# Scores and old states of a chunked retention in four 64x64 tiles of TensorE, with y in two banks

## The chip, the cores and the metric

The kernel runs on one core of a Trainium2 chip. The metric is the device time of one execution in microseconds (us); TensorE, VectorE, ScalarE and GpSimd are the core's engines, called PE (and PEld for its weight loads), DVE, ACT and POOL in the profile. All timed runs that are compared here are of the fast state, with a mean granted TensorE clock of 0.990 to 1.0 (below 0.993 only in load_early); one run of the kernel before, of 1494.38 us, was of the slow state and is left out. Two single looks have no state and are marked.

## The reference, cut to what matters

```python
# q, k, v: (4 batches, 8 heads, 768 positions, 64), float32
gamma = 1 - 2.0 ** (-5 - np.arange(H))
for t in range(S):
    state = gamma * state + k[t] (x) v[t]            # 64x64 a head
    y[t]  = 1/sqrt(64) * q[t] @ state
x = y as (3072 tokens, 512)
out = (silu(x @ w_gate) * (x @ w_val)) @ w_out       # d_ff = 1536
```

## The kernel before

The recurrence is cut into chunks of 128 positions. Of each chunk the kernel makes scores (keys x queries, decayed and masked), y as the sum of an attention part inside the chunk and of what the state before the chunk gives, and then the new state. Eight heads are four pairs; a pair's two heads lie in partitions 0-63 and 64-127. The tokens go through the two-layer network in four segments of 768 tokens, each of six chunks. The retention of segments 1 to 3 is done piece by piece between the matrix products of the segment before, in what I call its *down stage* (the second layer; a product there is 12 matmul records of 256 columns, 2.6 us). One such piece, a *step*, is: scores of the next chunk, y of this one, this one's state.

```python
def bank(tag):                       # PSUM has eight banks
    own = {"x": (0, 1), "wz": (2, 3), "s": (4, 5), "st": (6,), "y": (7,)}[tag]
    ...
def scores(c):
    kt, qt = (pairs(t) for t in chunks[c][:2])
    sp = [bank("s") for i in range(2)]
    for n in range(NP):              # 4 pairs
        for i in range(2):           # the pair's heads: 64 rows each
            r = ds(D * i, D)
            nc.tensor.matmul(sp[i][:, ts(n, P)], kt[r, n], qt[r, n], start=True, stop=True, ...)
    ...                              # VectorE: times the mask, into a[0], a[1]
def mix(c):
    ...
    if ci:                           # old states' part of y
        for n in range(NP):
            for i in range(2):
                r = ds(D * i, D)
                nc.tensor.matmul(y[r, ts(n, P)], prev[r, n], qd[r, n], start=(n == 0), ...)
    for n in range(NP):              # attention part
        for i in range(2):
            nc.tensor.matmul(y[ds(D * i, D), ts(n, P)], vn[:, ts(2 * n + i, D)], a[i][:, n], ...)
    nc.scalar.copy(xT[...], pairs(y))
def retention(s):                    # a step
    ...
        scores(cs[n + 1]); mix(cs[n]); decay(cs[n]); state(cs[n])
    ...
```

A matmul of 64 rows (contraction) and 128 output partitions runs in a 64x128 tile of the array, one of 64 rows and 64 output partitions in a 64x64 tile, one of 128 rows and 64 output partitions in a 128x64 tile.

## Time and profile before

| | before |
|---|---|
| time, median of the first three runs | 723.43 us (723.40 to 723.66) |
| TensorE busy | 707.4 us of a span of 722.3 |
| VectorE, ScalarE, GpSimd busy | 467.1, 239.8, 239.0 us |
| the three down stages with retention in them | 78.22, 74.55, 75.59 us |

The busy shares, the chain and the timeline of one step are in the prediction. Here are the three down stages (I take a stage from its first product's first matmul to the first matmul of the next stage). The view gives for each stretch its length, then busy us and number of instructions for PE, PEld, DVE, ACT and POOL, then the granted clock, the DMA share and GB/s:

```profile
144.20:222.42 78.22, 77.35 (x634) 65.81 (x632) 56.81 (x111) 12.32 (x35) 11.98 (x9) 1.00 0.64 237
320.69:395.24 74.55, 74.55 (x603) 64.20 (x602) 37.80 (x63) 12.80 (x37) 10.19 (x8) 1.00 0.39 131
492.49:568.08 75.59, 75.59 (x603) 64.85 (x602) 37.72 (x63) 12.35 (x35) 11.38 (x9) 1.00 0.38 130
```

By this view, which counts short gaps between pipelined records as busy, TensorE is busy for all of the second and third stretch and for all but 0.9 us of the first, so whatever these stages lose or gain is TensorE's own time.

### The profile page before, as it was taken

To read this page: it belongs to the slowest core of one execution; us is meant where nothing else is said; L and a number is where in the kernel's file an instruction comes from. 1 tells how busy PE (TensorE), PEld (TensorE's weight loads), DVE (VectorE), ACT (ScalarE), POOL (GpSimd) and SP (SyncE) were. 2 spreads that over 40 slices of the span, in tenths; PEclk is the share of its full clock that TensorE was granted. 3 is DMA by queue.
4 is the path that set the end of the run, shared out by engine and by line. 5 is a ranking of instruction groups with operands and counts; after the bars stand their busy time and mean duration, and the time that the engine had idled before them with its cause. 6 is when DMAs were issued, how large, how long until landed. Compare 5 with 4: busy or idle time off the path is not lost.

```text
span 722.3 us, 11724 instructions
## 1 busy us (share of the span) xinstructions
PE 707.4 (98%) x4544; PEld 616.0 (85%) x4544; DVE 467.1 (65%) x836; ACT 239.8 (33%) x484; POOL 239.0 (33%) x147
## 2 busy tenths in 40 slices
PE   7898999999999999999999999999999999999997
PEld 6654555678889999998888999998888999999886
DVE  3888998686858887875355575656652656667420
ACT  2668778411212232421122333331121233243000
POOL 1334444513101727470210445372210072735000
PEclk9999999999999999999999999999999999999999
DMA  9797986805997967742822555550473155530010
GB/s 319 257 375 255 290 289 220 312 15 192 395 347 277 332 206 271 244 164 88 259 92 103 183 202 206 203 177 16 135 260 132 63 196 202 202 132 1 9 51 30
DMA packets 60824, 139.06 MB, mean 193 GB/s; under 512 B 4576, under 2 KB 27616, under 8 KB 60768
## 3 DMA queue, kind: packets, MB, share of 16 engines
q1 hardware_dynamic: 57312, 132.01, 53.1%
q10 hardware_dynamic: 3456, 6.29, 2.3%
q8 instruction: 36, 0.59, 0.3%
q14 instruction: 20, 0.16, 0.1%
HBM read 101.72 MB, written 36.57 MB: 191 GB/s over the span
## 4 chain that ended last, share of the span: by engine, by line
PE 91%; DVE 1%; DMA 1%; ACT 1%; issue 1%; DVEq 0%; ACTq 0%
PE bank L626 40%; PE bank L709 26%; PE bank L515 13%; PE bank L718 4%; PE bank L385 3%; PE bank L446 3%; PE bank L442 2%; PE bank L424 1%; DMA hsp<-in_w_gate_dram 1%; DVE ring L289 0%; DVE iop L591 0%; ACT bank L246 0%; DVE hT L665 0%; ACT loadp L249 0%; DVE ring L261 0%
## 5 line engine op out<-in xcount | busy, mean ns | idle before, releaser
L626 PE MATMUL bank<-loadp,ring 128*128 128x192 f32 x720 | 140.3, 327 | 0.0
L709 PE MATMUL bank<-wot,hsp 128*128 128x256 f32 x576 | 129.8, 382 | 0.0
L709 PEld LDWEIGHTS bank<-wot,hsp 128*128 128x128 f32 x576 | 108.0, 190 | 15.8 <-issue 0.5
L626 PEld LDWEIGHTS bank<-loadp,ring 128*128 128x128 f32 x720 | 120.6, 190 | 1.0 <-ACT midp L591 0.7
L591 DVE TENSOR_TENSOR iop<-bank,iop 128x384 f32<-128x384 f32 x144 | 79.7, 556 | 56.3 <-PE bank L626 52.9
L626 PE MATMUL bank<-xs,ring 128*128 128x192 f32 x432 | 87.9, 326 | 0.0
L661 POOL TENSOR_TENSOR hT<-iop 128x768 f32<-128x768 f32 x36 | 67.0, 1862 | 34.8 <-DVE iop L591 34.8
L591 ACT COPY hsp<-bank 128x384 f32<-128x384 f32 x90 | 42.9, 478 | 100.3 <-PE bank L626 89.6
L626 PEld LDWEIGHTS bank<-xs,ring 128*128 128x128 f32 x432 | 73.2, 190 | 0.0
L591 POOL TENSOR_TENSOR iop<-hsp,midp 128x768 f32<-128x768 f32 x9 | 16.3, 1814 | 165.7 <-ACT hsp L591 137.2
L515 PE MATMUL bank<-xs,ring 128*128 128x384 f32 x192 | 64.7, 488 | 2.6 <-DVE xs L498 1.7
L626 PE MATMUL bank<-xT,ring 128*128 128x192 f32 x324 | 66.2, 327 | 0.7 <-DVE iop L591 0.7
L709 PE MATMUL bank<-wot,hT 128*128 128x256 f32 x288 | 65.5, 381 | 0.0
L515 PEld LDWEIGHTS bank<-xs,ring 128*128 128x128 f32 x192 | 36.1, 190 | 29.4 <-issue 2.3
L709 PEld LDWEIGHTS bank<-wot,hT 128*128 128x128 f32 x288 | 54.3, 190 | 7.6 <-issue 0.2
L626 PE MATMUL bank<-hsp,ring 128*128 128x192 f32 x288 | 56.7, 326 | 0.5 <-ACT hsp L591 0.5
L626 PEld LDWEIGHTS bank<-xT,ring 128*128 128x128 f32 x324 | 54.8, 190 | 2.0 <-DVE iop L591 1.8
L515 PE MATMUL bank<-xT,ring 128*128 128x384 f32 x144 | 49.4, 488 | 1.6 <-DVE hT L552 1.6
L626 PEld LDWEIGHTS bank<-hsp,ring 128*128 128x128 f32 x288 | 48.4, 190 | 0.8 <-ACT hsp L591 0.8
L591 DVE TENSOR_TENSOR midp<-bank,midp 128x384 f32<-128x384 f32 x72 | 39.8, 554 | 13.8 <-PE bank L626 12.4
L768 DVE TENSOR_TENSOR iop<-bank,iop 128x256 f32<-128x256 f32 x12 | 5.1, 424 | 65.1 <-PE bank L709 48.1
L449 ACT COPY xT<-bank 128x512 f32<-128x512 f32 x24 | 14.1, 586 | 97.3 <-PE bank L446 97.3
(146 smaller groups left out, 985.9 us busy)
## 6 DMA issues: line engine op xcount, KB each, us to landing
ring<-unitt SPq DMA_DIRECT2D x50, 896.0 KB, 4.6
unitt<-ring SPq DMA_DIRECT2D x21, 896.0 KB, 6.4
unitb<-ring SPq DMA_DIRECT2D x12, 896.0 KB, 7.2
ring<-unitb SPq DMA_DIRECT2D x21, 512.0 KB, 6.0
out_dram<-iop ACTq DMA_DIRECT2D x24, 256.0 KB, 2.4
loadp<-in_w_val_dram SPq DMA_DIRECT2D x18, 256.0 KB, 3.8
loadp<-in_w_gate_dram SPq DMA_DIRECT2D x9, 512.0 KB, 6.1
midp<-in_w_out_dram SPq DMA_DIRECT2D x12, 256.0 KB, 6.1
```

What stands on the lines that cost most here:

```text
L385: nc.tensor.matmul(sp[i][:, ts(n, P)], kt[r, n], qt[r, n], start=True, stop=True, skip_group_check=True)
L424: nc.tensor.matmul(st[ds(D * i, D), n], kd[:, h], vn[:, h], start=(n == 0), stop=True, skip_group_check=True)
L442: nc.tensor.matmul(y[r, ts(n, P)], prev[r, n], qd[r, n], start=(n == 0), stop=False, skip_group_check=True)
L446: nc.tensor.matmul(y[ds(D * i, D), ts(n, P)], vn[:, ts(2 * n + i, D)], a[i][:, n], start=(ci == 0 and n == 0), stop=True, skip_group_check ...
L449: nc.scalar.copy(xT[:, :, c // NCK % 2, ts(ci % L, P)], pairs(y))
L515: nc.tensor.matmul(o, w[:, slot, k], a[:, k], start=(start and k == 0), stop=(stop and k == KH - 1), skip_group_check=True)
L591: events.append((t, len(events), lambda: fn(*args, **kw)))
L626: nc.tensor.matmul(o[:, h], w[:, h, slot], rhs, start=(start and h == 0), stop=True, skip_group_check=True)
L661: by_block(9.5, 13.5, lambda r: pool(to[:, r], u2[:, r], p5[:, r], op=add))
L709: nc.tensor.matmul(o, a[:, k], wot[k][:, slot], start=(start and k == 0), stop=(k == FH - 1), skip_group_check=True)
L718: nc.tensor.matmul(o, a_dn(0, 0, u)[:, k], wot[k][:, B11], start=(k == 0), stop=(k == FH - 1), skip_group_check=True)
L768: tt(ev[0][:, DH:], wb, u2, op=ALU.add)
```

## The change

The intent: use all four quarters of the array for old states (before, row half 0 went to column half 0 and row half 1 to column half 1), give scores the same tile shape so that the array does not change its mode between the two, and pay for it with a second bank for y and with ScalarE copies that move each head to its place. Comments, blank lines and what the first segment keeps are cut.

```diff
-        own = {"x": (0, 1), "wz": (2, 3), "s": (4, 5), "st": (6,), "y": (7,)}[tag]
+        own = {"s": (4, 5), "y": (6, 7)}[tag]
@@ scores
         for n in range(NP):
-            for i in range(2):
-                r = ds(D * i, D)
-                nc.tensor.matmul(sp[i][:, ts(n, P)], kt[r, n], qt[r, n],
-                                 start=True, stop=True, skip_group_check=True)
+            for m in (slice(None),) if c in first_chunks else (slice(0, D), slice(D, P)):
+                for i in range(2):
+                    r = ds(D * i, D)
+                    nc.tensor.matmul(sp[i][m, ts(n, P)], kt[r, n, m], qt[r, n],
+                                     start=(n == 0), stop=True, skip_group_check=True)
@@ state
-        st = bank("st")[:, : NP * D].rearrange("p (n e) -> p n e", n=NP)
+        st = banks[6 if c in first_chunks[:4] else 3][:, : NP * D]
@@ mix, later segments
+            y = [bank("y")[:, : 2 * P].rearrange("p (b t) -> p b t", b=2) for i in range(2)]
+            own = [(2 * h + b, i, h, y[i][:, b])
+                   for b in range(2) for i in range(2) for h in range(2)]
+        for k, (n, i, h, to) in enumerate(own if ci else []):
+            r = ds(D * i, D)
+            nc.tensor.matmul(to[ds(D * h, D)], prev[r, n], qd[r, n],
+                             start=k < 2 * len(y), stop=False, skip_group_check=True)
...                                      # attention part: same targets
-        nc.scalar.copy(xT[:, :, c // NCK % 2, ts(ci % L, P)], pairs(y))
+            for h in range(2):
+                for i in range(2):
+                    nc.scalar.copy(xT[ds(D * i, D), ds(2 * h, 2), seq, pos],
+                                   y[i][ds(D * h, D)])
@@ down stage, twice
-            z = bank("wz")[:, :DH]
+            z = banks[2][:, :DH]
```

More of the change, by code (lines that the diff above doesn't have):

```diff
@@ L419, in state @@
         new = state_of(c)
-        st = bank("st")[:, : NP * D].rearrange("p (n e) -> p n e", n=NP)
+        st = banks[6 if c in first_chunks[:4] else 3][:, : NP * D]
+        st = st.rearrange("p (n e) -> p n e", n=NP)
         for n in range(NP):
@@ L431, in mix @@
     def mix(c):
-        ci = c % NCK
+        ci, seq, pos = c % NCK, c // NCK % 2, ts(c % L, P)
         qd, vn = pairs(chunks[c][1]), chunks[c][2]
         a = att.pop(c)
-        y = banks[(0, 1, 2, 3, 7, 6)[first_chunks.index(c)]] if c in first_chunks else bank("y")
-        if ci:
-            prev = state_of(c, 1)
-            for n in range(NP):
-                for i in range(2):
-                    r = ds(D * i, D)
-                    nc.tensor.matmul(y[r, ts(n, P)], prev[r, n], qd[r, n],
-                                     start=(n == 0), stop=False, skip_group_check=True)
-        for n in range(NP):
-            for i in range(2):
-                nc.tensor.matmul(y[ds(D * i, D), ts(n, P)], vn[:, ts(2 * n + i, D)],
-                                 a[i][:, n], start=(ci == 0 and n == 0), stop=True,
-                                 skip_group_check=True)
-        nc.scalar.copy(xT[:, :, c // NCK % 2, ts(ci % L, P)], pairs(y))
-        if c in first_chunks:
-            att[c] = pairs(y)
+        prev = state_of(c, 1)
+        if c in first_chunks:
+            y = [pairs(banks[(0, 1, 2, 3, 7, 6)[first_chunks.index(c)]])]
+            own = [(n, i, i, y[0][:, n]) for n in range(NP) for i in range(2)]
+        else:
+            y = [bank("y")[:, : 2 * P].rearrange("p (b t) -> p b t", b=2) for i in range(2)]
[5 more added lines that the diff above has]
+                             start=k < 2 * len(y), stop=False, skip_group_check=True)
+        for k, (n, i, h, to) in enumerate(own):
+            nc.tensor.matmul(to[ds(D * h, D)], vn[:, ts(2 * n + i, D)], a[i][:, n],
+                             start=(ci == 0 and k < 2 * len(y)), stop=True,
+                             skip_group_check=True)
+        if c in first_chunks:
+            att[c] = y[0]
+            nc.scalar.copy(xT[:, :, seq, pos], att[c])
+        else:
+            for h in range(2):
+                for i in range(2):
+                    nc.scalar.copy(xT[ds(D * i, D), ds(2 * h, 2), seq, pos],
+                                   y[i][ds(D * h, D)])
     def retention(s):
@@ L757, in down @@
         cur = dict(hs)
-        wb = bank("wz")[:, :DH]
+        wb = banks[2][:, :DH]
         product(wb, T1, cur[1])
```

## The prediction

> **What bounds the kernel now.** I read the page's busy shares first, then the chain that ended last, then the list of waits, then a timeline of one step of the changed code.
>
> ```profile
> PE 707.4 (98%) x4544; PEld 616.0 (85%) x4544; DVE 467.1 (65%) x836; ACT 239.8 (33%) x484; POOL 239.0 (33%) x147
> PE 91%; DVE 1%; DMA 1%; ACT 1%; issue 1%; DVEq 0%; ACTq 0%
> PE bank L626 40%; PE bank L709 26%; PE bank L515 13%; PE bank L718 4%; PE bank L385 3%; PE bank L446 3%; PE bank L442 2%; PE bank L424 1%; DMA hsp<-in_w_gate_dram 1%; DVE ring L289 0%; DVE iop L591 0%; ACT bank L246 0%; DVE hT L665 0%; ACT loadp L249 0%; DVE ring L261 0%
> ```
>
> TensorE is busy 98% of the span and is 91% of the chain; VectorE and ScalarE have 35% and 67% to spare. Of the lines that the change touches, scores (L385), the attention part of y (L446), the old states' part (L442) and the state update (L424) are together 9% of the chain, some 65 us, and a fair part of it is the first segment, which keeps its instructions. The list of waits has no TensorE entry on these lines that is worth anything over 3.6 us in the whole run. So they cost what their instructions take to stream, plus gaps that are TensorE's own. The gaps show in the timeline of one step (scores of the next chunk, then y of this one, then its state), TensorE matmuls alone; columns are start, length, line, tiles, form, count:
>
> ```profile
> 164.96 0.59 PE L709 MATMUL bank<-wot,hsp 128*128 128x256 f32 x2
> 165.48 1.16 PE L385 MATMUL bank<-loadp 64*128 64x128 f32 x16
> 166.57 1.09 PE L442 MATMUL bank<-loadp,state 64*64 64x128 f32 x16
> 167.59 1.09 PE L446 MATMUL bank<-midp,loadp 128*64 128x128 f32 x16
> 168.52 0.64 PE L424 MATMUL bank<-loadp 128*64 128x64 f32 x16
> 169.08 0.48 PE L709 MATMUL bank<-wot,hT 128*128 128x256 f32 x1
> ```
>
> Each of these calls is two records (16 records for 8 calls), since every f32 product is two matmuls. The view of L442 by duration adds the length of one record, 269 ns as a rule, which is modelled and overlaps the next; so I take starts.
>
> ```profile
> L442 PE MATMUL bank<-loadp,state x160: 269/269/320, 166.6 to 543.8; 64*64 64x128 f32 x160
> L446 PE MATMUL bank<-midp,loadp x192: 272/273/323, 167.6 to 544.8; 128*64 128x128 f32 x192
> ```
>
> From the timeline, L442's last record starts at 166.57+1.09-0.27 = 167.39. The individual records lie in pairs 7 ns apart, one for each head of a pair, and the next pair follows 109 ns later (111 ns in L385). A 256-column product outside takes 216 ns from start to start, 0.84 ns a column, so 128 columns stream in 107-108 ns: two tiles run side by side, and each keeps its own pace. L442's rows 0-63 go to columns 0-63 and rows 64-127 to columns 64-127: half of the array stands idle.
>
> **What the Trainium skill says.** (1) "TensorEngine Tiling (Array Packing)", Key Properties: a change of tiling mode drains TensorE, a change of tile alone doesn't. The trace agrees: L385, L442 and L446 differ in mode, and between the end of one's streaming and the next one's weight load there is 0.09 us each time (L442's last record streams until 167.39+0.11 = 167.50, L446 begins at 167.59), while L446 and L424, of one mode, follow without a gap. After the gap the first weights are not hidden: 0.05 us for 64 columns, 0.11 us for 128 (the first records are 0.05 and 0.10 us longer than the rest). (2) The same page, Restrictions and Gotchas, Gotcha 1: different row tiles may not write one PSUM bank at a time. That is why y now needs two banks; before, the diagonal gave each head its own partitions of one bank. Nothing in this trace tests it. (3) "TensorE: Matmul & The Clock Gate", Part 1: start to start never drops below about 25 ns. Four tiles of 128 columns need 109/4 = 27 ns. The densest stretch of this trace, L424, has 16 records with 58 ns from pair to pair, 29 ns each, so 27 ns is just outside what is shown here. (4) "ScalarE: Activation LUTs", What ACT_TABLE_LOAD costs: an activation with immediates takes 186 ns + 0.833 ns an element; 512 elements give 613, the trace has 586 (below), and 372 for a copy of 256 elements (L722), against 399.
>
> **The change, part by part.** It touches the 18 chunks of segments 1 to 3; the trace has 96 records of L385 in each of these three segments, 64 of L442 in the middle one (its first two chunks have no old state) and 96 in the others.
>
> Scores: 16 records in two 64x128 tiles become 32 in four 64x64 tiles. The streaming per tile is the same, 8 records. Before: gap 0.09, first weights 0.11, 8 x 0.111 = 0.89, sum 1.09 us. After, if four tiles run as freely as two: 0.09 + 0.05 + 8 x 0.109 = 1.02. I choose 115 ns a round of four instead of 109, since 27 ns a record is near the floor: 0.09 + 0.05 + 0.92 = 1.06. Gain 0.03 us each, 18 times: 0.5 us (1.3 at best).
>
> Old states: before 0.09 + 0.05 + 8 x 0.109 = 1.02 us (166.57 less 0.09 to 167.50). After: four tiles, 4 rounds x 0.115 = 0.46, and no gap and no bare weights where scores go before, since both are in 64x64 tiles. Gain 0.56 us. Of the 16 chunks with old states, 13 follow scores; the last of each segment has no scores before it and keeps the gap, gain 0.42. Sum 13 x 0.56 + 3 x 0.42 = 8.5 us.
>
> Attention part of y and states: same number, shape and mode; the state goes to bank 3. Nothing.
>
> ScalarE: one copy of 128x512 becomes four of 64x256, and copies for chunks of the first segment stay.
>
> ```profile
> L449 ACT COPY xT<-bank 128x512 f32<-128x512 f32 x24 | 14.1, 586 | 97.3 <-PE bank L446 97.3
> ```
>
> At 0.37 us each, as a copy of 256 elements takes, four are 1.5 us for 0.59, so up to 0.9 us later for each chunk and at most 16 us more on an engine that is 67% idle. What reads them is the sums of x on VectorE, one 2.6 us product later or more; the decay of the state, behind them on ScalarE, is done at 170.3 in the step above and wanted at 175.5. TensorE's next write into y comes after the state (0.5 us), a product (2.6 us) and the scores (1 us), so 4 us later, and the copies need some 1.5. Beside other work, free.
>
> Banks: the second output half's product and the first's now share bank 2. Between the two there is always a whole product of 2.6 us in bank 0 or 1. VectorE's emptying is late by at most about 1 us where it is busiest:
>
> ```profile
> 217.24 5.34 PE L709 MATMUL bank<-wot,hT 128*128 128x256 f32 x24
> ...
> 220.63 0.42 DVE L729 TENSOR_TENSOR iop<-bank,iop 128x256 f32<-128x256 f32 x1
> ```
>
> The product that L729 empties ends at 219.8, the emptying at 221.05, the next product ends at 222.4. Free, with more than 1 us in hand.
>
> Sum: 0.5 + 8.5 = 9.0 us with my 115 ns, 10.2 us at 109 ns. All of it lies on the chain. 723.4 - 9.0 = 714.4; between the two cases I say 714.
>
> **The rivals.** (a) Four tiles don't run four abreast: issue, or weight loads of tiles with the same rows, hold them to two at a time. Then the 32 records of scores take 16 rounds, 1.75 us for 0.89, 18 x 0.81 = +14.6 us, and only 13 gaps of 0.15 are won: about 736. For it: no stretch of this trace has four tiles. Against it: row tiles (L385) and column tiles (L446) each run side by side here, weights included, and a tile that waits doesn't hold up the other: at 11.36 us the second column tile, which had waited for VectorE, and the first tile's next call start 7 ns apart. With three abreast scores would lose 0.22 us each and old states win 0.44 or 0.29: about 721.
> (b) Another wait takes the place: y's two banks serve one chunk, so four copies must be out before the next y; or one bank for two products. If each of the 16 steps lost 0.5 us, 722. The margins above, 2.5 and 1 us, speak against it.
> (c) The second-level products start earlier than their operands are ready, most of all after the first down stage, where VectorE is busy 57 of 80 us with weight sums and waits up to 3.7 us for their DMA. It would eat at most that stage's third of the gain: 717. Against it: no matmul waits there now, and the sums of the units end some microseconds before they are wanted.
>
> **Range and chances.** The arithmetic allows 10.2 us at most, so 712 is about the floor once run-to-run noise (0.3 us) is added; overheads of issue or (b) or (c) in part give up to 719. Range 711.5 to 719.5. Faster by over 2% would take 14.5 us, more than all that the change can win: 0.02. Slower by over 2% needs all of (a) and something more: 0.03. Within 2%: 0.95.
>
> **What would show it.** In the trace after: L385's 32 records in about 0.9 us and old states' 16 in about 0.45, right behind, with rounds of four starts 109 to 115 ns apart; no 0.09 us gap between them; the gap before the attention part still there; 3.4 us saved in each down stage (2.3 in the middle one); ScalarE up by 10 to 16 us; no wait of TensorE for a copy to xT or for L729. I am wrong if rounds of four take over 150 ns, or if a matmul waits for ScalarE or for bank 2.

## The result, and the profile after

| | before | after |
|---|---|---|
| median, first measurement | 723.54 us (4 runs) | 714.59 us (4 runs, 714.15 to 716.40) |
| ratio of the fast runs | | 0.9873, 95% interval 0.9845 to 0.9901 |
| span of the profiled run | 722.3 us | 712.4 us |
| TensorE busy, records | 707.4 us, 4544 | 698.0 us, 4832 |
| ScalarE busy | 239.8 us | 257.2 us |
| down stages | 78.22, 74.55, 75.59 us | 74.53, 72.03, 71.90 us |
| the rest of the span | 493.92 us | 493.92 us |

Ratios are the mean time of one kernel's fast runs over that of the other's of the same rounds, so not quite the ratio of the medians quoted. The gain is 1.3%: clear of noise, but by the 2% rule of this study the two kernels count as the same. Run times of one kernel vary by more than a microsecond here. Where two traces of one kernel were kept (the changed kernel, causal, copies_x2), the three stages differ by 0.03 to 0.56 us in sum and the rest of the span by 0.1 to 3.8 us. The two traces of the table differ by 9.90 us, and all 9.90 are in the three stages (3.69 + 2.52 + 3.69); that the rest agrees to 0.01 us is a lucky pair (in after_again it is 493.78). The profiled run of before was a slightly long one (724.06 us) and that of after a short one (714.15), hence 8.95 between the medians. For shares of the change I use stage lengths. Those of the second and third stage repeat to 0.01 us; the first varies by half a microsecond, most of it a wait that a second trace, shown below, has.

Page of the changed kernel, busy shares and chain:

```profile
PE 698.0 (98%) x4832; PEld 607.8 (85%) x4832; DVE 467.6 (66%) x836; ACT 257.2 (36%) x538; POOL 239.8 (34%) x147
PE 91%; DVE 1%; DMA 1%; ACT 1%; issue 1%; SPq 0%; DVEq 0%; ACTq 0%
PE bank L640 40%; PE bank L723 27%; PE bank L529 13%; PE bank L732 4%; PE bank L388 3%; PE bank L455 3%; DMA hsp<-in_w_gate_dram 1%; PE bank L428 1%; PE bank L452 1%; DVE ring L290 0%; DVE iop L605 0%; ACT bank L247 0%; DVE hT L679 0%; ACT loadp L250 0%; SPq L221 0%
```

The bound is what it was. Line numbers have moved: scores are L388 now, old states L452 (2% of the chain before, 1% now), attention L455, state L428, the down products L723. The three stages, in the view of the stretches:

```profile
144.19:218.72 74.53, 73.66 (x729) 62.67 (x728) 57.46 (x110) 18.01 (x53) 11.98 (x9) 1.00 0.66 245
317.00:389.03 72.03, 72.03 (x699) 61.90 (x698) 37.15 (x63) 18.67 (x55) 10.25 (x8) 1.00 0.39 136
486.27:558.17 71.90, 71.90 (x698) 61.72 (x697) 37.66 (x63) 18.05 (x53) 11.48 (x9) 1.00 0.38 136
```

TensorE has some 95 records more in each stretch and is done sooner; in this trace no new wait of it appears. ScalarE has 5.7 to 5.9 us more in each. The same step as in the prediction, TensorE's matmuls in the timeline of the changed kernel:

```profile
164.89 0.59 PE L723 MATMUL bank<-wot,hsp 128*128 128x256 f32 x2
165.42 1.10 PE L388 MATMUL bank<-loadp 64*64 64x128 f32 x32
166.34 0.62 PE L452 MATMUL bank<-loadp,state 64*64 64x128 f32 x16
166.89 1.09 PE L455 MATMUL bank<-midp,loadp 128*64 128x128 f32 x16
167.81 0.64 PE L428 MATMUL bank<-loadp 128*64 128x64 f32 x16
168.38 0.48 PE L723 MATMUL bank<-wot,hT 128*128 128x256 f32 x1
```

From the first start of scores to the next product it was 165.48 to 169.08, 3.60 us, and is 165.42 to 168.38, 2.96 us. Thirty-two records of scores take 0.92 us up to old states' first start, and sixteen of old states 0.55 up to the attention part with the gap in it, for 1.02 before. In the single records the four tiles of a round start 7 ns after one another and the next round 109 ns after this one: 27 ns a record, without loss. The waits of TensorE's loads on these lines (columns: us in total, times, longest) hold no ScalarE; the largest are of the kind that the kernel before had, where L385 had 3.6 us and L446 2.9:

```profile
PEld bank L388 <- issue: 4.5, 14, 0.3
PEld bank L455 <- issue: 3.3, 19, 0.2
```

ScalarE's copies in the same step: four in 1.51 us, and the decays behind them.

```profile
167.81 1.51 ACT L464 COPY xT<-bank 64x256 f32<-64x256 f32 x4 [8.33 <-PE bank L455]
169.35 1.06 ACT L414 ACTIVATE state<-state,tab 128x64 f32<-128x64 f32 x4
```

TensorE writes old states into these banks again at 174.68 (the single records), 5.4 us after the last copy has ended.

### The profile page after: what moved, and what is told of

The parts are those of the page before. It is cut to its first block, busy times and chain, and to the rows that moved or that the text cites. A ratio compares the mean times of both kernels' runs of the same rounds, so it can differ in the third digit from the quotient of the medians.

```text
span 712.4 us, 12349 instructions
## 1 busy us (share of the span) xinstructions
PE 698.0 (98%) x4832; PEld 607.8 (85%) x4832; DVE 467.6 (66%) x836; ACT 257.2 (36%) x538; POOL 239.8 (34%) x147
## 4 chain that ended last, share of the span: by engine, by line
PE 91%; DVE 1%; DMA 1%; ACT 1%; issue 1%; SPq 0%; DVEq 0%; ACTq 0%
PE bank L640 40%; PE bank L723 27%; PE bank L529 13%; PE bank L732 4%; PE bank L388 3%; PE bank L455 3%; DMA hsp<-in_w_gate_dram 1%; PE bank L428 1%; PE bank L452 1%; DVE ring L290 0%; DVE iop L605 0%; ACT bank L247 0%; DVE hT L679 0%; ACT loadp L250 0%; SPq L221 0%
## 5 line engine op out<-in xcount | busy, mean ns | idle before, releaser
L723 PE MATMUL bank<-wot,hsp 128*128 128x256 f32 x576 | 129.8, 382 | 0.0
L723 PEld LDWEIGHTS bank<-wot,hsp 128*128 128x128 f32 x576 | 108.0, 190 | 15.9 <-issue 1.0
L529 PE MATMUL bank<-xs,ring 128*128 128x384 f32 x192 | 64.7, 488 | 2.4 <-DVE xs L512 1.7
L723 PE MATMUL bank<-wot,hT 128*128 128x256 f32 x288 | 65.5, 381 | 0.0
L529 PEld LDWEIGHTS bank<-xs,ring 128*128 128x128 f32 x192 | 36.1, 190 | 29.2 <-issue 2.3
L723 PEld LDWEIGHTS bank<-wot,hT 128*128 128x128 f32 x288 | 54.3, 190 | 7.6 <-DVE midp L394 0.2
L640 PEld LDWEIGHTS bank<-xT,ring 128*128 128x128 f32 x324 | 54.8, 190 | 2.0 <-DVE iop L605 1.8
L464 ACT COPY xT<-bank 64x256 f32<-64x256 f32 x72 | 26.4, 366 | 68.3 <-PE bank L455 67.4
L529 PE MATMUL bank<-xT,ring 128*128 128x384 f32 x144 | 49.4, 488 | 1.6 <-DVE hT L566 1.6
L529 PEld LDWEIGHTS bank<-xT,ring 128*128 128x128 f32 x144 | 27.0, 190 | 21.2 <-DVE hT L566 2.2
```

Source lines behind the costliest of these rows:

```text
L464: nc.scalar.copy(xT[ds(D * i, D), ds(2 * h, 2), seq, pos], y[i][ds(D * h, D)])
L529: nc.tensor.matmul(o, w[:, slot, k], a[:, k], start=(start and k == 0), stop=(stop and k == KH - 1), skip_group_check=True)
L640: nc.tensor.matmul(o[:, h], w[:, h, slot], rhs, start=(start and h == 0), stop=True, skip_group_check=True)
L723: nc.tensor.matmul(o, a[:, k], wot[k][:, slot], start=(start and k == 0), stop=(k == FH - 1), skip_group_check=True)
```

## The experiments

All kernels gave correct results. My theory: the 9.9 us are the halved streaming of old states plus TensorE's own gaps and bare weight loads, and the rest of the change is free. The rivals: the gain is mostly in scores; the banks, or the copies, matter; the tiles are only free of one another in a lucky order.

### scores_two: scores back in two tiles

```diff
-            for m in (slice(None),) if c in first_chunks else (slice(0, D), slice(D, P)):
+            for m in (slice(None),):
```

> The changed kernel with scores back in two 64x128 tiles, all else kept. Theory (the gain is streaming of the old states halved, plus TensorE's own gaps): each of 18 scores loses 0.07 us (bare weights of 128 columns again, 111 for 109 ns a round) and the 13 old states that follow scores get back the gap of 0.15 us, so 3.2 us of the 9.9 us between the two traces are lost: about 717.7 us, the three down stages about 1.2, 0.9 and 1.2 us longer than in the changed kernel. Rival (the gain is mostly in scores, or in the banks): nearly all is lost, 723, or nothing, 714.5.

Measured: 717.46 us (6 runs), ratio to before 0.9905 (0.9888 to 0.9922). The stages are 75.68, 72.85 and 73.05 us: 1.15, 0.82 and 1.15 more than in the changed kernel, 3.12 in all, 3.2 expected. A step in its timeline:

```profile
167.43 1.16 PE L388 MATMUL bank<-loadp 64*128 64x128 f32 x16
168.53 0.67 PE L452 MATMUL bank<-loadp,state 64*64 64x128 f32 x16
169.12 1.09 PE L455 MATMUL bank<-midp,loadp 128*64 128x128 f32 x16
```

Scores take 1.10 us up to the next line for 0.92, since the gap is back, and the records of old states take longer again (0.67 for 0.62), for their first weights are bare. So about a third of the gain hangs on scores being in 64x64 tiles, although they stream as long as before. Two things are in that third, and the stages tell them apart: each has six scores, and 5, 3 and 5 of them stand before old states. From 1.15 = 6a + 5b and 0.82 = 6a + 3b, b, the cost of a change of shape before old states, is 0.165 us, 2.1 us in 13 places, and a, scores' own smaller weights and rounds, 0.05 us, 1.0 us in 18 places.

### y_diag: y as before, scores in four tiles

```diff
-            y = [bank("y")[:, : 2 * P].rearrange("p (b t) -> p b t", b=2) for i in range(2)]
-            own = [(2 * h + b, i, h, y[i][:, b]) for b in range(2) for i in range(2) for h in range(2)]
+        y = bank("y")                          # mix() as in the kernel before
+                    nc.tensor.matmul(y[r, ts(n, P)], prev[r, n], qd[r, n], ...)
+        nc.scalar.copy(xT[:, :, c // NCK % 2, ts(ci % L, P)], pairs(y))
```

> The changed kernel with y as before: old states on the diagonal in one bank, one copy of 128x512; scores stay in four tiles. Theory: only the streaming is lost, 16 x 4 rounds x 0.109 = 7.0 us, for diagonal and four tiles are one mode, so no gap comes back: about 721.4 us. The two losses of this run and of scores_two add up to the whole, 10.2 us. Rival (a change of which tiles are used costs as much as a change of mode): another 13 x 0.1 = 1.3 us, 722.7. Rival (the gain is mostly in scores): 715.

Measured: 721.31 us (5 runs), ratio 0.9959 (0.9945 to 0.9974). Stages 77.13, 73.76 and 74.50 us: 2.60, 1.73 and 2.60 more, 6.93 in all, 7.0 expected.

```profile
165.44 1.10 PE L388 MATMUL bank<-loadp 64*64 64x128 f32 x32
166.36 1.05 PE L446 MATMUL bank<-loadp,state 64*64 64x128 f32 x16
167.34 1.09 PE L450 MATMUL bank<-midp,loadp 128*64 128x128 f32 x16
```

Scores and old states follow each other without a gap, so two diagonal tiles and four tiles are one mode; sixteen records in two tiles take 0.98 us up to the attention part for 0.55. The losses of the two runs are 3.12 + 6.93 = 10.05 us, the whole is 9.90: the parts add up, and no part of the gain needs another cause. This run has one copy, the changed kernel four, which is one more sign that the copies are not on the path.

### banks_copies: the old matmuls, the new banks and copies

```diff
# mix() as in y_diag, scores as in scores_two, and
-        nc.scalar.copy(xT[:, :, c // NCK % 2, ts(ci % L, P)], pairs(y))
+            for h in range(2):
+                for i in range(2):
+                    nc.scalar.copy(xT[ds(D * i, D), ds(2 * h, 2), c // NCK % 2, ts(ci % L, P)],
+                                   pairs(y)[ds(D * i, D), ds(2 * h, 2)])
```

> The matmuls of the kernel before, with the banks of the changed one (one bank for two products, the state in bank 3, y in turn in two) and ScalarE's four copies of 64x256. Theory: banks and copies are free, neither cost nor gain: 723.5 us, the down stages as long as before to 0.1 us, ScalarE's busy time up by 14 to 17 us. Rival (the banks of y or of the products were a hidden wait before): down to 720. Rival (the copies cost something): up to 726.

Measured: 724.39 us against 724.30 of before in the same rounds, ratio 1.0005 (0.9992 to 1.0018). The stages are 78.22, 74.54 and 75.59 us, those of before to 0.01. ScalarE is busy 257.6 us, 17.8 more, a little over the range given. Banks and copies in this form neither cost nor bring anything. Here y takes its two banks in turn, one a chunk, while the changed kernel needs both for each chunk, so this run gives the copies more room than they have there; that they are free in the changed kernel too rests on its trace, where no matmul waits for them.

### tile_by_tile: another order of the calls

```diff
-        for n in range(NP):
-            for m in ...:
-                for i in range(2):
+        for m in ...:
+            for i in range(2):
+                for n in range(NP):
+        by_tile = own if c in first_chunks else sorted(own, key=lambda o: (o[1], o[2], o[0]))
+        for k, o in enumerate(by_tile if ci else []):          # old states, tile after tile
```

> The changed kernel with the order of calls changed: scores and old states one tile after another (all calls of a tile in a row) instead of going round the four tiles. Theory A (a tile's queue runs far ahead of the others): nothing changes, 714.5. Theory B (the look-ahead across tiles is short, a few records): tiles run one after the other in whole or in part; with none abreast scores would take 32 x 0.109 = 3.5 us for 0.9 and old states 1.7 for 0.44, 18 x 2.6 + 16 x 1.3 = +68 us, so something between 730 and 782.

Measured: 741.75 us (4 runs), ratio 1.0246 (1.0224 to 1.0268). Stages 83.31, 80.80 and 80.68 us, 8.8 more each. (The first segment's scores are in the new order too; it costs under 1 us there.)

```profile
167.61 2.24 PE L388 MATMUL bank<-loadp 64*64 64x128 f32 x29
169.59 0.35 PE L455 MATMUL bank<-loadp,state 64*64 64x128 f32 x3
169.69 0.27 PE L388 MATMUL bank<-loadp 64*64 64x128 f32 x1
169.75 0.30 PE L455 MATMUL bank<-loadp,state 64*64 64x128 f32 x3
```

Twenty-nine of the 32 records of scores fill the time up to 169.59, and three more come among those of old states, by then on the other three tiles. In the single records, the second tile's first one starts at 168.105, just after the fifth of the first tile (168.099), the third tile's at 168.599, just after the fifth of the second (168.594): a tile's stream is passed only when it has three records left to start. So theory B holds, in the lower part of its range: the look-ahead is real but short. A tile's eight records take 0.87 us and the next tile's start 0.49 us after its own, so that 1.8 tiles run at a time, and in this order the change would have been a loss of 2.5%.

### two_calls: two calls of a tile in a row

```diff
+        runs = ((0,), (1,), (2,), (3,)) if c in first_chunks else ((0, 1), (2, 3))
+        for m, i, ns in [(m, i, ns) for ns in runs for m in ms for i in range(2)]:
+            for n in ns:
+        # old states as in tile_by_tile: each tile has just two calls
```

> The changed kernel with two calls (four records) of a tile in a row before the next tile's turn, in scores and old states of the later segments. In tile_by_tile the second tile began when the first one's fifth record did, so with three of its records waiting. Theory A (each tile may have three or so of its own waiting): four abreast as before, 714.6. Theory B (three or so may wait over all tiles together): the second tile starts at once, the third and fourth 0.2 and 0.3 us later, each section 0.2 to 0.4 us longer, 34 sections: 721 to 728.

Measured: 716.50 us (4 runs), ratio 0.9883 (0.9856 to 0.9909). Stages 75.21, 72.60 and 72.58 us, 0.6 to 0.7 more than in the changed kernel.

```profile
166.07 1.17 PE L390 MATMUL bank<-loadp 64*64 64x128 f32 x32
166.99 0.74 PE L457 MATMUL bank<-loadp,state 64*64 64x128 f32 x16
167.66 1.09 PE L460 MATMUL bank<-midp,loadp 128*64 128x128 f32 x16
```

Scores take 0.92 us up to old states' first start, as in the changed kernel; in the single records the four tiles start 13 ns apart and then keep their 109 ns, with one slip of 0.05 us of three of them at the second turn. So the limit is one of each tile, not of all together, and four records in a row just fit. Theory A holds but for about 0.1 us a step.

### copies_x2, copies_x4 and copies_x2_again: how much room ScalarE has

```diff
-            for h in range(2):
+            for h in list(range(2)) * 2        # and * 4
```

> The changed kernel with each of the four copies of y made twice. Theory (ScalarE has room: in the trace the four take 1.5 us from 167.8 on, and TensorE writes y again at 174.7): no change, 714.6 give or take a run, no wait of TensorE for ScalarE in the down stages. Rival (the copies are near the path): each of 18 steps loses up to 1.5 us, up to 741.

> The changed kernel with each of the four copies of y made four times, 16 copies or 6.1 us a step. Theory: this uses up the room; the copies end at 173.9 in that step, the state's decay behind them at 174.9, its add on VectorE at 175.5, while TensorE wants state and banks at 174.7; products' own copies wait behind them too. One to two us lost in each of about 16 steps: 730 to 747, with TensorE waiting for ScalarE or VectorE. If it is still 714.6, the room is larger than I read it.

Single looks, state unknown. Twice: 715.58 us; the second and third stage are unchanged (72.03 and 71.90), the first is 76.04, 1.51 more. Its timeline near the end of that stage:

```profile
216.87 0.42 DVE L786 TENSOR_TENSOR iop<-bank,iop 128x256 f32<-128x256 f32 x1
...
217.35 1.35 PE L723 MATMUL bank<-wot,hT 128*128 128x256 f32 x5 [0.82 <-DVE iop L786]
```

VectorE's list is long here, and L786, which empties the bank of the next product, stands at the end of it; TensorE waits 0.82 us. A smaller delay of 0.17 us stands 3.7 us earlier, behind L782. In the changed kernel's trace L786 is done at 215.55 and the product that needs the bank starts at 216.1, so 0.6 us are in hand.

Four times: 729.90 us, stages 83.65, 76.60 and 74.07, that is 15.9 more in all. The expectation (1 to 2 us in each of about 16 steps, 730 to 747) is missed by 0.1 us at its low end, and its form is not what happened: three waits make most of it.

```profile
178.72 1.86 PE L723 MATMUL bank<-wot,hsp 128*128 128x256 f32 x6 [2.07 <-DVE iop L743]
```

L743 empties bank 2, the one that two products share now; TensorE stood for 2 us. What follows a little later, in the view of the stretches:

```profile
179.90:182.80 2.90, 2.90 (x8) 2.29 (x7) 1.48 (x3) 2.75 (x9) 0.00 (x0) 0.50 0.95 254
```

The granted clock (the number after the counts) is 0.50 in this stretch, and the single records of products lie 0.43 us apart for 0.22. In the clock records of the trace the half clock lasts from 179.84 to 183.26, 3.4 us, so the wait cost its length and then some 1.7 us more (seven gaps longer by 0.21 and two by less). Two more waits, of 2.61 us (for L786) and 2.21 us (for ScalarE, which empties bank 2 in another product), are followed by 3.4 us of half clock too; the three with what follows are, if each cost 1.7 us more like the first, some 12 of the 15.9 us.

Was it the copies that cost the first stage 1.5 us in copies_x2, or a chance delay? The changed kernel itself, run a second time beside causal_again (below), also had a wait at the same place, 0.46 us beyond the usual distance of two starts, in a first stage of 75.09 us for 74.53, after VectorE had waited for the DMA of weight units:

```profile
210.94 0.69 DVE L171 TENSOR_TENSOR ring<-ring 128x512 f32<-128x512 f32 x1 [3.48 <-DMA ring<-unitb]
...
216.38 0.92 PE L723 MATMUL bank<-wot,hT 128*128 128x256 f32 x3 [0.30 <-DVE iop L786]
```

> The kernel of copies_x2, unaltered. Its first look lost 1.5 us in the first down stage, behind an emptying on VectorE that was late. But after_again, with single copies, has a wait of 0.46 us at the same place, and in both VectorE had waited for the DMA of weight units just before. Theory (the room of ScalarE is enough, the loss was the DMA's): the first stage lies within 74.5 to 75.1 us, as in the changed kernel. Rival (the doubled copies did it): 76.0 again.

Measured: 718.62 us (4 runs), ratio 0.9919 (0.9903 to 0.9936); the first stage is 76.00, with waits of 0.31 and 0.80 us at the same two places. So the rival holds, by two traces against two: the doubled copies did it; how they make VectorE later was not followed further. The rest of this run's extra time lies before the first down stage, where no copy is doubled yet (see the end of the experiments). The copies are free as they are, in two stages even when doubled, but in the first stage there is no room for twice as many.

### load_early: the weight units' loads one ahead

```diff
-            if count[1] < len(to_sum) + 1 and k > 1 and count[1] < 3 + count[2] // 3:
+            if count[1] < len(to_sum) + 1 and k > 1 and count[1] < 4 + count[2] // 3:
```

> The changed kernel with the loads of weight units in the first down stage issued one unit earlier (4 ahead for 3). Theory (VectorE's waits of 1.2 to 3.5 us for these loads make it late for emptying a product's bank, with 0.6 us in hand): the waits shrink, no matmul waits at the end of the stage, 74.5 us for the stage, 714.3 with less scatter. Rival (a load starts when its place in the ring is free, whatever the order): the same waits, the stage 74.5 to 75.1 as before, 714.6.

Measured: 732.38 us (4 runs), ratio 1.0115 (1.0096 to 1.0134); the first stage is 88.99 us, the other two unchanged. Neither expectation is met. VectorE's waits for these loads did not shrink but grew to 22.4 us in all, the longest 7.8 us:

```profile
224.00 0.69 DVE L171 TENSOR_TENSOR ring<-ring 128x512 f32<-128x512 f32 x1 [4.90 <-DMA ring<-unitb]
225.53 0.42 DVE L782 TENSOR_TENSOR iop<-bank,iop 128x256 f32<-128x256 f32 x1
...
226.00 1.22 PE L723 MATMUL bank<-wot,hT 128*128 128x256 f32 x2 [7.90 <-DVE iop L782]
```

The waits of the DMA queue itself between 180 and 228 us show why the loads came later (L161 issues a load, L176 stores a unit that is done); the changed kernel first, then this run:

```profile
SPq L161 <- DMA unitt<-ring: 12.0, 7, 3.6
SPq L161 <- DMA unitt<-ring: 37.0, 6, 7.7
```

A load waits until the unit in its place of the ring is stored. With one load more ahead, the next store stands right behind that waiting load (a load at 205.45, a store at 205.88; 213.19 and 213.65; 219.56 and 220.02), so each load waits for the whole store before it, and the last loads go out 6.4 to 7.7 us apart, for 3.4 to 5.3 in the changed kernel. What the run also shows, much enlarged, is the way from a late load to TensorE: VectorE stands waiting for the load, empties the product's bank late, and TensorE stands still.

### causal, and causal_again beside after_again: a shorter version

Scores of keys 64 to 127 with queries 0 to 63 are multiplied by zeros of the mask. With scores in quarters, these calls can stream half the columns. So that both column halves of the array gain, odd pairs keep their keys with the halves exchanged (a layout of k, v, decays and mask on the host).

```diff
+                    late = c not in first_chunks and (m.start > 0) != (n % 2 > 0)
+                    t = slice(D, P) if late else slice(0, P)
-                    nc.tensor.matmul(sp[i][m, ts(n, P)], kt[r, n, m], qt[r, n],
+                    nc.tensor.matmul(pairs(sp[i])[m, n, t], kt[r, n, m], qt[r, n, t],
```

> The changed kernel, with the scores that the mask zeroes anyway left out: keys 64 to 127 of a chunk need only queries 64 to 127, so half of the 64x64 tiles' calls stream 64 columns for 128. For odd pairs of heads the two halves of the keys change places (rows of k, v, their decays and the mask, laid out so on the host), so that each tile has as many short calls as long ones. Theory (a tile's own stream sets the time, tiles are free of one another): a scores section takes 4 x 0.109 + 4 x 0.058 = 0.67 us for 8 x 0.109 = 0.87, 18 x 0.21 = 3.7 us less than the changed kernel: 710.9, each down stage 1.2 us shorter. Rival (issue is near its limit with four tiles, so shorter streams gain nothing): 714.6, same down stages.

> The kernel of the run causal, unaltered, in the same rounds as the changed kernel: its three down stages were 1.2 us shorter each in the trace, so 3.6 us less than after_again, ratio 0.982 to the kernel before. If it is within 1 us of after_again, the gain of the stages is lost elsewhere.

> The changed kernel itself, unaltered, as the neighbour of causal_again in the same rounds: 714.6 by the first measurement, ratio to the kernel before 0.987.

Measured: causal 712.30 us, ratio to before 0.9840 (0.9820 to 0.9861). In its second time, in the same rounds, 712.68 us and 0.9835 (0.9808 to 0.9862) against after_again's 714.59 us and 0.9854 (0.9832 to 0.9877). Stages of causal: 73.34, 70.81 and 70.68 us, 1.19, 1.22 and 1.22 less than the changed kernel's, as expected (1.2). A step of it:

```profile
165.74 0.90 PE L390 MATMUL bank<-loadp 64*64 64x128 f32 x32
166.46 0.62 PE L454 MATMUL bank<-loadp,state 64*64 64x128 f32 x16
```

Scores take 0.72 us for 0.92. So even rounds of mixed length, 32 records in 0.7 us or 22 ns each, are not held up by issue. In the timed runs the gain over the changed kernel is 1.9 us between the medians, less than the stages' 3.6, and the two intervals overlap; both kernels' runs scatter by 2 to 5 us (causal_again from 710.67 to 715.23). It is the fastest kernel of the study by every median and by the stages, but against the changed kernel the timed difference is not clear of noise. Part of the scatter is the first stage (73.34 and 73.71 us in causal's two traces, 74.53 and 75.09 in the changed kernel's); another part lies before the first down stage, whose first product starts between 143.9 and 147.8 us in the traces of all these kernels. Most of that is there by 36 us: the first product of the network (L515 before, L529 in the changed kernel) starts between 32.3 and 35.3 us, after waits of TensorE in the first segment, a good part of them for loads of q. The latest is copies_x2_again, where one such wait takes 2.86 us, for 1.2 to 1.3 in most of the others, and 3.4 us of half clock follow. Why these loads scatter stays open.

## Why the prediction was right or wrong

The time was right: 714.0 said, 714.59 measured, in the range. Step by step:

- **The bound.** Right. TensorE stayed at 98% and 91% of the chain, and what it saved in the three stages reached the end: the rest of the span is 493.92 us in both traces (to this digit by luck).
- **Scores.** Right in kind, too small. With 115 ns a round I had 0.03 us each; at the measured 109 ns it is 0.07 (1.09 before; 165.325, the end of the last product's streaming, to 166.343 after, 1.02). This is the term that was mis-sized, out of caution about a floor at 25 ns a record that 27 ns did not touch and that causal's 22 ns show to be no floor here. The prediction's own trace spoke against reading that figure across tiles: two tiles' records start 7 ns apart there.
- **Old states.** Right: y_diag gives back 6.93 us, where four rounds of 109 ns saved 16 times are 7.0. The gap between scores and old states went, the one before the attention part stayed (166.80 to 166.89), both as said.
- **The sum.** 9.0 said, 10.2 as the best case; the traces have 9.90, stages 3.69, 2.52 and 3.69 where I said 3.4, 2.3 and 3.4. The same 109 for 115 ns explains it to 0.3 us (208 rounds by 6 ns is 1.2 us). Between the medians it is 8.95, nearer to 9.0 by chance of the runs.
- **Copies.** Free, as said (the changed kernel's trace; banks_copies). ScalarE's extra was 17.4 us, over the 16 of the text. The room was larger than I said: I put one product between a step and the next write into y, there are two, 6.9 us from the first copy's start for 4.
- **Banks.** Free, as said. The narrowest place was not the one that I looked at (bank 2, over 1 us) but the next product's own bank, 0.6 us in hand behind the same list of VectorE, where copies_x2 waits. With four times the copies bank 2 does become a wait, the rival (b) of the prediction. Under (2) the prediction says that nothing in its trace tests the rule on row tiles and banks. The kernel before does in part: in old states rows 0-63 and rows 64-127 write one bank, in different partitions, 7 ns apart, and y_diag does so again with correct results. Four tiles in one bank would also write the same partitions, and no run tries that.
- **The rivals.** (a) fell: four tiles run four abreast. But tile_by_tile shows how near it was: the same calls in another order are rival (a) in part, at 741.75 us where (a) said 736. The prediction took from the trace that a waiting tile does not hold up another, and misread it: the first tile's last record before that point starts at 10.977 us and has streamed by 11.09, yet its next call, which stands behind the waiting one in the program, starts only with it, at 11.36. So it was held up for 0.27 us, and the point was no evidence against (a). In tile_by_tile a tile's records pass another's only when no more than three of those wait. (b) did not occur. (c) occurs in a small part, and in some runs: VectorE's DMA waits in the first stage (1.2 and 2.8 us in one trace of the changed kernel, 1.8 and 3.5 in the other, up to 3.7 before) are as long as before while TensorE comes earlier, and in the second trace TensorE waits 0.46 us, of which the first had nothing. It takes 0.56 us of 9.9 there, where (c) as I put it took 3.4.

## What to carry to other kernels

When half of the array idles in a mode, look for the same work in the other quarters, and give its neighbours the same tile shape even if they stream no faster: a third of this gain came from that, two thirds of it from the change of shape that fell away and one third from scores' own smaller weights. Issue the calls round the tiles, at most two f32 calls of a tile in a row, for four records nearly fit (0.1 us a step) and eight do not. Moving work to an idle engine is free only as far as the waits behind it have room, which a run with the work doubled, and repeated, can show.

## What the Trainium skill lacked or had wrong

- "TensorEngine Tiling (Array Packing)" says that a change of mode drains TensorE but gives no cost: here 0.09 us of gap, and 0.05 or 0.11 us of weights that are not hidden (64 or 128 columns). Two diagonal 64x64 tiles and four are one mode (y_diag).
- No page says how far a tile may run ahead: in tile_by_tile a tile's stream is passed by others only when three or fewer of its records wait; eight in a row cost 8.8 us a stage, four 0.6 to 0.7 (tile_by_tile, two_calls).
- "TensorE: Matmul & The Clock Gate", Part 3, has matmuls start in strict program order, and weights overlap only where the row groups differ. In the tile_by_tile trace three records of old states (L455) start from 169.59 on and one of scores (L388), earlier in the program, at 169.69; and in the attention part two column tiles with the same rows keep rounds of 109 ns, weight loads included, where weights that are not hidden cost 0.05 us.
- The same page, Part 1, gives a floor of about 25 ns from start to start, without a word on tiles there. It is no floor across tiles: records of different tiles start 7 ns apart, and causal's scores have 32 records in 0.72 us, 22 ns each. It puts the return to the half clock after an idle window of about 3.4 us; in copies_x4 waits of 2.07, 2.61 and 2.21 us were each followed, about 1 us after TensorE had gone on, by 3.4 us at a granted clock of 0.50.
- "ScalarE: Activation LUTs", What ACT_TABLE_LOAD costs, has back-to-back activations overlap by about 93 ns. The decays do (332 ns each, 239 apart). The copies of 64x256 out of PSUM, listed as COPY in the trace, don't (363 to 368 ns each, 375 to 393 apart); the page has no figure for them.
